# Seven products for every pair's second matrix, and the first MLP for all blocks ahead of the second

## The chip, the cores and the metric

The kernel runs on one core of a Trainium2 chip. The metric is device time in microseconds (us) from launch to end. The kernel before takes 1684.14 us, the median of three runs (1682.77, 1684.14, 1688.67).

## The reference

Attention over 8 batches, 8 heads, 576 tokens and head size 64, with a softmax of q over its features and a softmax of k over the sequence, is followed by two MLPs on 4608 tokens of width 512:

```python
x = attention(q, k, v)                       # 4608 x 512
x = relu(x @ w_in)**2 @ w_out                # w_in 512 x 2048, w_out 2048 x 512
x = (sigmoid(x @ w_gate) * (x @ w_val)) @ w_out2   # d_ff 1536
```

The weights arrive as float64. The result is float32.

## The kernel before, in words

**Arithmetic.** Each float32 operand is split into a rounded part and a rest (`hi_of` on ScalarE, L210, records of L211; `lo_of` on VectorE, L213, records of L214). `mm3` (L216) makes one product from three matmuls (L217 to L219). A seven-product form of Strassen's kind multiplies a 2x2 arrangement of blocks with seven products in place of eight: sums of operand blocks are made ahead (`plan_b` L673 and `b_comb` L669, records of L671, for activations; `plan_sums` L342 for weights), and each product's result is copied out of or added to an SBUF tile (`plan_seven` L762, records of L733, L211, L728). The order of the products is `PRODUCTS` (L137).

**Blocks and stages.** The tokens form nine blocks of 512. Blocks 0 to 2 go through the first MLP one at a time, beside the preparation of the first MLP's weights (until 366 us). The others go in pairs: `IN` is (3,4), (5,6), (7,8), called in0, in1, in2 here. `in_stage` (L1105) has two halves of the hidden width; in each, two units of seven products against w_in (`plan_in` L1036) are followed by the products against w_out. For these there are two forms. Eight products (L1158 to L1196, `o_mm` L854, `o_ev` L872): each of eight groups of the pair (4 `kk` in 2 halves) has four operand tiles split, and a weight tile that was fetched serves both blocks, 16 fetches of 0.5 MB a pair. Seven products (`out_seven` L1065, `p_o` L864): each group has seven tiles split and four sums made, each weight tile serves one product, 28 fetches, and the results of the second half are added to those of the first, loaded back (`o_ld7` L896). `OUT7` (L176) names the pairs that take seven. The first MLP's result goes to DRAM.

`GATE` is (0,1), (2,3), (4,5), (6,7), (8). `gate_stage` (L1200) loads a pair of blocks back and runs the second MLP on it, with seven products throughout.

**What sets the order.** Nothing is issued in the order of the loops. Every piece of work is put in a list with a key (a time in us by the plan's own clock), the engines that may do it and their costs, what it comes after, and which tiles it takes and gives back (`Plan.add` L44). `Plan.trace` (L55) runs through it as a list scheduler: an engine that is free takes the ready work with the lowest key for which tiles are there. The order that comes out is issued, and each engine's queue keeps it. A key is a priority, not an earliest time. Weight loads, weight fetches and the splits of a stage keep their own order by chains (L1309). `SIZES` (L177) gives the tiles: 11 of "W" for fetched and prepared weights and raw loads, 6 of "S" for split operands of the second matrices, 6 of "a" for attention's transposed q and for results on their way out, 5 of "w".

`STAGES` (L1275) is the order in which stages get their keys, one behind another from T1 = 358; a stage's length in keys is worked out from its matmuls. `BESIDE` (L1288) says beside which entry of `STAGES` the attention of which pair of blocks is planned (`plan_blocks` L1002; `plan_k` L601 and `plan_q` L622 give its steps). The nine matrices of the second MLP are prepared by `plan_w` (L390): each is four raw loads, a rounding of float64 to float32 words on ScalarE and VectorE (L250 to L284), four sums, seven splits and seven stores. Their keys are spread evenly from T4 = 299.6 to 40 past the start of the first gate stage (L1297).

Loads, fetches and stores are all issued by SyncE.

Of the kernel before, what the change touches and what calls it, by code (L numbers as in the profile page):

```python
# [29 lines left out]
class Plan:  # L30
# [13 lines left out]
    def add(self, key, engines, name, fn, *args, after=(), take=(), give=(), slack=0.0):  # L44
        n = len(self.ops)
        assert name not in self.names, name
        self.names[name] = n
        self.ops.append((key, n, engines, name, fn, args, tuple(after), tuple(take), tuple(give), slack))
# [94 lines left out]
def attention_mlp_mlp(  # L143
# [29 lines left out]
    F2 = w_out2.shape[0]  # L173
    wide = w_in.dtype == I64

    OUT7 = (2,)  # L176
    SIZES = {"X": 14, "W": 11, "S": 6, "f": 19, "x": 8, "q": 3, "a": 6, "w": 5, "k": 2, "v": 2, "km": 1, "kr": 2, "pa": 2, "qm": 4, "qr": 4}  # L177
    cst = ctx.enter_context(tc.tile_pool(name="cst", bufs=1))
    p4 = ctx.enter_context(tc.tile_pool(name="p4", bufs=1))
# [182 lines left out]
    def plan_first(kind, g, times, tag):  # L362

        ready, own = {}, {}
        for b in range(4) if kind == "in" else (0, 2, 1, 3):
# [5 lines left out]
            if kind == "in":  # L371
                add(t - 3.9, {DMA: 0.8}, ("w32", kind, g, b), w_store32, (kind, g, b), after=done)
                end.append(("w32", kind, g, b))
            if kind == "in" or not OUT7:
                add(t - 3, {FREE: 0.0}, ("wfre", kind, g, b), lambda: None, after=end, give=[tag])
# [297 lines left out]
    def plan_b(nm, ready, times, tag, n, gives):  # L673


        us = AS if n > 256 else 0.32
        ub = VEC if n > 256 else {DVE: 0.34}
        lo = lambda i: ("blo", nm, i)
        cb = lambda x: ("bcb", nm, x)

        def split(i, b, after, give=()):
            add(times[i], {ACT: us}, ("bhi", nm, i), b_hi, nm, i, b, tag, n, after=after, take=[tag])
            add(times[i] + 0.1, ub, lo(i), b_lo, nm, i, b, CHOSEN, after=[("bhi", nm, i)], give=give)

        def comb(x, i, o, a, b, after, give=()):
            add(times[i] - 1.5, ub, cb(x), b_comb, nm, o, a, b, CHOSEN, after=after, give=give)

        split(1, "11", ready["11"])
        comb("T1", 5, "11", "12", "11", [lo(1), *ready["12"]])
        split(5, "11", [cb("T1")])  # L690
        comb("T3", 7, "12", "22", "12", [cb("T1"), *ready["22"]])
        comb("T2", 6, "11", "22", "11", [lo(5), *ready["22"]])
        split(6, "11", [cb("T2")])
        split(2, "21", ready["21"])
        split(7, "12", [cb("T3")], gives.get("12", ()))
        split(3, "22", [*ready["22"], cb("T2"), cb("T3")], gives.get("22", ()))
        comb("T4", 4, "21", "21", "11", [lo(2), lo(6), cb("T2")], gives.get("11", ()))
        split(4, "21", [cb("T4")], gives.get("21", ()))
# [303 lines left out]
    def plan_blocks(js, t, per):  # L1002

        for j in js:
            new = [b for _, b in segs(j) if b not in done_b]
            done_b.update(new)
            for p in range(NP):
                for b in new:
                    plan_k(b, p, t, 1.0, x_before.get(j, []))
                plan_q(j, p, t + 2, 1.0)  # L1010
                t += per / NP
# [50 lines left out]
    IN = [tuple(range(j, j + 2)) for j in range(NONE, NB, 2)]  # L1062
    GATE = [(j, j + 1) for j in range(0, NB - 1, 2)] + [(NB - 1,)]
# [41 lines left out]
    def in_stage(n, t):  # L1105
# [5 lines left out]
        for h in range(2):  # L1111
# [15 lines left out]
            for kk in range(4):  # L1127
                nm = G + (kk,)
                if n not in OUT7:
                    continue  # L1130
# [9 lines left out]
                plan_b(nm, ready, times, "S", nt, {qn: ["f"] for qn in ready})  # L1140
            if n in OUT7:
                sorder.extend(("bhi", G + (kk,), i) for i in PRODUCTS for kk in range(4))
            for kk in range(4):
                if n in OUT7:
                    break
                for qn, (name, where) in gready[kk].items():
# [8 lines left out]
                    add(tk + 0.1, LOW, ("blo", nm, qn), b_lo, nm, qn, qn, CHOSEN, after=[("bhi", nm, qn)], give=["f"])  # L1155
            if n not in OUT7:
                sorder.extend([("bhi", G + (kk,), f"{r + 1}{tq + 1}") for tq in range(2) for kk in range(4) for r in range(2)])
            if n in OUT7:  # L1158
                t = out_seven(n, h, js, G, t)
# [112 lines left out]
        freed[prs[0]] = (t, fin)  # L1272
        return t

    STAGES = [(in_stage, 0), (in_stage, 1), (gate_stage, 0), (gate_stage, 1), (in_stage, 2), (gate_stage, 2), (gate_stage, 3), (gate_stage, 4)]  # L1275
    before = []
    for stage, n in STAGES:
        if stage is in_stage:
# [6 lines left out]
    plan_blocks([2], T2 + 6, TS1 * F1 - 30)  # L1285
    plan_blocks(IN[0], T3 + 5, (T1 - T3 - 40) / 2)

    BESIDE = {0: 1, 3: 2}  # L1288
    t = T1
    for i, (stage, n) in enumerate(STAGES):  # L1290
        if i in BESIDE:
            js = IN[BESIDE[i]]
            plan_blocks(js, t + 4, ((D1 if stage is in_stage else D2_) - 60) / len(js))
# [76 lines left out]
```

## Time and profile before

| | |
|---|---|
| median of three runs | 1684.14 us |
| the profiled execution's own time | 1689.22 us |
| its span, first to last instruction | 1687.4 us |
| mean granted TensorE clock | 0.992 |
| in0 (366.2 to 558.9 us), attention of blocks 5 and 6 beside it | 192.7 us |
| in1 (558.9 to 722.1 us) | 163.2 us |
| gate 0 (722.1 to 904.2 us) | 182.1 us |
| gate 1 (904.2 to 1096.8 us), attention of blocks 7 and 8 beside it | 192.6 us |
| in2 (1096.8 to 1248.3 us), seven products | 151.5 us |
| gate 2 (1248.3 to 1424.5 us) | 176.2 us |

Gates 3 and 4 follow until the end. The limits of the stages are the starts of their first matmuls; at some of them a few matmuls of two stages are interleaved. Busy time of an engine in a window is the union of its instructions' records. A window that shows an engine busy all the time does not say that it runs at its peak, since records of consecutive instructions overlap; the distance from start to start does.

### The profile page before, as it was taken

The page shows a single profiled execution, that of the slowest core. Times are in us where ns is not written, and L with a number is a line of the kernel's source. Part 1 is how long each engine was busy: PE and PEld are TensorE (multiplying, and loading weights), DVE is VectorE, ACT ScalarE, POOL GpSimd, SP SyncE. Part 2 cuts the span into 40 slices and gives each one's busy share as a digit, 9 for nine tenths or more (in the row PEclk, how much of TensorE's full clock was granted, in tenths as well). Part 3 has the DMA queues.
Part 4 walks back from the last instruction along what each step waited for, and adds up shares of the span by engine and source line. Part 5 has one row for each costly group of instructions (what it writes and reads, how often), then busy time and mean ns, then how long its engine had stood idle before and what let it go on. Part 6 is the DMA issues. An engine that isn't in the chain of part 4 may idle for free.

```text
span 1687.4 us, 24273 instructions
## 1 busy us (share of the span) xinstructions
PE 1651.6 (98%) x8740; PEld 1416.2 (84%) x8740; DVE 1158.9 (69%) x2178; ACT 927.6 (55%) x1632; POOL 1.9 (0%) x14
## 2 busy tenths in 40 slices
PE   6899999999999999999999999999999999999999
PEld 4677788878888888888898889988888899889998
DVE  8988846788889656865774758665954583448446
ACT  5876645567477657643454556464733453335344
POOL 0000000000000000000000000000000000000000
PEclk9998999999999999999999999999999999999999
DMA  7998899798897979899567555867786667555796
GB/s 287 343 359 327 305 360 334 278 342 343 298 347 256 369 256 351 303 335 355 188 191 243 191 186 164 274 201 250 243 291 195 191 210 240 191 196 185 246 377 253
DMA packets 153175, 457.90 MB, mean 271 GB/s; under 512 B 16096, under 2 KB 25312, under 8 KB 153056
## 3 DMA queue, kind: packets, MB, share of 16 engines
q1 hardware_dynamic: 153056, 456.36, 77.4%
q8 instruction: 69, 1.13, 0.3%
q14 instruction: 50, 0.41, 0.1%
HBM read 360.35 MB, written 95.94 MB: 270 GB/s over the span
## 4 chain that ended last, share of the span: by engine, by line
PE 90%; DVE 5%; DMA 2%; ACT 2%; issue 1%; SPq 0%; ACTq 0%; DVEq 0%
PE bank L217 29%; PE bank L219 28%; PE bank L218 28%; PE kps L467 2%; PE xps L577 2%; DMA ws<-w_in 1%; DVE bX L214 0%; DMA wraw<-in_moe_w_out_dram 0%; DVE whl L214 0%; DVE bS L214 0%; DMA kt<-in_k_dram 0%; DVE xf L671 0%; PE qsw L524 0%; DVE wf L277 0%; DVE s L671 0%
## 5 line engine op out<-in xcount | busy, mean ns | idle before, releaser
L217 PE MATMUL bank<-bX,ws 128*128 128x512 f32 (+1 forms) x1176 | 447.2, 380 | 3.2 <-DMA ws<-w_in 3.2
L218 PE MATMUL bank<-bX,ws 128*128 128x512 f32 (+1 forms) x1176 | 441.3, 375 | 0.0
L219 PE MATMUL bank<-bX,ws 128*128 128x512 f32 (+1 forms) x1176 | 441.2, 375 | 0.0
L733 DVE TENSOR_TENSOR s<-s,bank 128x512 f32<-128x512 f32 (+1 forms) x285 | 184.4, 652 | 206.6 <-PE bank L219 170.6
L211 ACT ACTIVATE s<-bank 128x512 f32<-128x512 f32 (+1 forms) x285 | 161.4, 570 | 225.9 <-PE bank L219 223.5
L217 PEld LDWEIGHTS bank<-bX,ws 128*128 128x128 f32 x1176 | 222.4, 189 | 42.3 <-ACT bS L211 3.5
L219 PEld LDWEIGHTS bank<-bX,ws 128*128 128x128 f32 x1176 | 222.1, 189 | 40.4
L218 PEld LDWEIGHTS bank<-bX,ws 128*128 128x128 f32 x1176 | 222.5, 189 | 37.9 <-issue 0.7
L211 ACT ACTIVATE bS<-s 128x512 fp32r<-128x512 f32 (+1 forms) x298 | 174.9, 598 | 124.4 <-PE bank L219 113.0
L214 DVE TENSOR_TENSOR bS<-s,bS 128x512 fp32r<-128x512 f32 (+1 forms) x298 | 191.6, 652 | 57.5 <-ACT bS L211 57.0
L217 PE MATMUL bank<-ws,bS 128*128 128x256 f32 x756 | 214.7, 284 | 0.0
L219 PE MATMUL bank<-ws,bS 128*128 128x256 f32 x756 | 214.1, 283 | 0.4 <-DVE bS L214 0.4
L218 PE MATMUL bank<-ws,bS 128*128 128x256 f32 x756 | 214.0, 283 | 0.0
L752 ACT ACTIVATE s<-s 128x512 f32<-128x512 f32 (+1 forms) x120 | 70.5, 589 | 140.2 <-DVE s L733 139.9
L217 PEld LDWEIGHTS bank<-ws,bS 128*128 128x128 f32 x756 | 145.0, 192 | 1.4 <-ACT s L211 0.3
L218 PEld LDWEIGHTS bank<-ws,bS 128*128 128x128 f32 x756 | 145.0, 192 | 1.0 <-issue 0.2
L219 PEld LDWEIGHTS bank<-ws,bS 128*128 128x128 f32 x756 | 145.0, 192 | 0.6 <-DVE bS L214 0.6
L217 PE MATMUL bank<-bS,ws 128*128 128x512 f32 x368 | 144.6, 393 | 0.2 <-issue 0.2
L218 PE MATMUL bank<-bS,ws 128*128 128x512 f32 x368 | 143.3, 389 | 0.0
L219 PE MATMUL bank<-bS,ws 128*128 128x512 f32 x368 | 143.3, 389 | 0.0
L211 ACT ACTIVATE whl<-wf 128x512 fp32r<-128x512 f32 x127 | 78.3, 626 | 50.1 <-DVE wf L284 27.8
L214 DVE TENSOR_TENSOR whl<-wf,whl 128x512 fp32r<-128x512 f32 x127 | 85.9, 689 | 10.1 <-ACT whl L211 9.9
(118 smaller groups left out, 2425.3 us busy)
## 6 DMA issues: line engine op xcount, KB each, us to landing
ws<-w_gv SPq DMA_DIRECT2D x210, 512.0 KB, 4.4
ws<-w_out SPq DMA_DIRECT2D x197, 512.0 KB, 4.3
ws<-w_in SPq DMA_DIRECT2D x116, 512.0 KB, 6.1
w_out<-whl SPq DMA_DIRECT2D x53, 512.0 KB, 4.7
w_gv<-whl SPq DMA_DIRECT2D x42, 512.0 KB, 6.2
w_in<-whl SPq DMA_DIRECT2D x32, 512.0 KB, 4.9
wraw<-in_moe_w_out_dram SPq DMA_DIRECT2D x28, 512.0 KB, 6.6
vt<-in_v_dram SPq DMA_DIRECT2D x32, 325.0 KB, 6.5
```

The costliest lines, as they stand in the source:

```text
L211: nc.scalar.activation(out=dst, in_=src, func=AF.Copy)
L214: by_name[engine].tensor_tensor(out=dst, in0=src, in1=hi.bitcast(F32), op=ALU.subtract)
L217: nc.tensor.matmul(ps, ah, bh, start=first, stop=False, skip_group_check=True)
L218: nc.tensor.matmul(ps, ah, bl, start=False, stop=False, skip_group_check=True)
L219: nc.tensor.matmul(ps, al, bh, start=False, stop=last, skip_group_check=True)
L467: nc.tensor.matmul(ps[:, 0:2 * D + 1], kt[:, r, :], vt[:, r, 0:2 * D + 1], start=(r == 0), stop=(r == RK - 1))
L577: nc.tensor.matmul(ps[:, e], kvf[b % 2][p], t[:, e], start=True, stop=True)
L733: nc.vector.tensor_tensor(out=t, in0=t, in1=banks[pr[b]][:, 0:n], op=ALU.add)
L752: nc.scalar.activation(out=t, in_=t, func=AF.Sigmoid)
```

## The change

`OUT7` names all three pairs, so in0 and in1 take seven products against w_out. `STAGES` puts the three in stages first and the five gate stages behind them. `BESIDE` plans the attention of blocks 7 and 8 beside in1 (entry 1) in place of gate 1 (entry 3). The keys of the nine matrices' preparation follow from the formula on L1297, which reads the start of the first gate stage.

```diff
-    OUT7 = (2,)
+    OUT7 = (0, 1, 2)
...
-    STAGES = [(in_stage, 0), (in_stage, 1), (gate_stage, 0), (gate_stage, 1), (in_stage, 2), (gate_stage, 2), (gate_stage, 3), (gate_stage, 4)]
+    STAGES = [(in_stage, n) for n in range(len(IN))] + [(gate_stage, n) for n in range(len(GATE))]
...
-    BESIDE = {0: 1, 3: 2}
+    BESIDE = {0: 1, 1: 2}
```

## Rows read from the trace of the kernel before

**Rows 1.** The page, part 1: busy time, share, instructions of each engine.
```profile
PE 1651.6 (98%) x8740; PEld 1416.2 (84%) x8740; DVE 1158.9 (69%) x2178; ACT 927.6 (55%) x1632; POOL 1.9 (0%) x14
```

**Rows 2.** The page, part 2: VectorE's busy tenths in 40 slices of 42.2 us.
```profile
DVE  8988846788889656865774758665954583448446
```

**Rows 3.** Waits of TensorE, 330 to 1690 us: total, times, longest.
```profile
PE bank L217 <- DMA ws<-w_in: 3.2, 1, 3.2
PE bank L217 <- DMA ws<-w_out: 1.2, 1, 1.2
```

**Rows 4.** Windows: length; busy PE, PEld, DVE, ACT, POOL; granted clock; DMA share, GB/s.
```profile
366.20:415.60 49.40, 46.25 (x208) 37.91 (x207) 36.52 (x74) 34.87 (x64) 0.00 (x0) 0.93 0.91 352
415.60:468.90 53.30, 53.30 (x264) 44.62 (x262) 46.85 (x105) 31.45 (x57) 0.00 (x0) 1.00 0.88 308
468.90:515.40 46.50, 46.50 (x231) 38.73 (x230) 38.16 (x83) 35.33 (x66) 0.00 (x0) 1.00 0.95 335
515.40:558.90 43.50, 43.50 (x194) 36.02 (x193) 36.77 (x64) 24.11 (x44) 0.00 (x0) 1.00 0.81 283
558.90:597.00 38.10, 38.10 (x170) 31.56 (x169) 23.50 (x38) 28.55 (x50) 0.00 (x0) 1.00 1.00 353
597.00:640.50 43.50, 43.50 (x194) 36.02 (x193) 26.07 (x45) 20.92 (x35) 0.00 (x0) 1.00 0.74 269
640.50:678.60 38.10, 38.10 (x170) 31.55 (x169) 26.47 (x45) 30.84 (x55) 0.00 (x0) 1.00 0.95 348
678.60:722.10 43.50, 43.50 (x194) 36.02 (x193) 35.12 (x61) 23.62 (x43) 0.00 (x0) 1.00 0.85 304
...
1096.80:1248.30 151.50, 151.26 (x668) 124.90 (x668) 100.73 (x161) 89.35 (x153) 0.00 (x0) 1.00 0.73 243
904.20:1096.80 192.60, 192.24 (x1114) 167.77 (x1113) 132.07 (x245) 104.53 (x164) 0.00 (x0) 1.00 0.63 208
1248.30:1424.50 176.20, 176.20 (x1016) 156.21 (x1015) 99.50 (x156) 75.49 (x125) 0.00 (x0) 1.00 0.66 212
722.10:904.20 182.10, 182.10 (x1045) 161.18 (x1043) 115.33 (x187) 85.86 (x143) 0.00 (x0) 1.00 0.75 264
```

**Rows 5.** Lines by form, VectorE: instructions that evict the first MLP's results.
```profile
L883 DVE TENSOR_TENSOR xp<-xp,bank 128x512 f32<-128x512 f32 x16 | 10.5, 692 | 6.2 <-DMA xp<-xp 4.8 <-PE bank L219 1.3
...
L733 DVE TENSOR_TENSOR xp<-xp,bank 128x512 f32<-128x512 f32 x14 | 9.0, 684 | 9.1 <-PE bank L219 9.1
...
L879 DVE COPY xo<-bank 128x512 f32<-128x512 f32 x6 | 4.1, 686 | 0.1
```

**Rows 6.** Timeline of VectorE in in0: start, length, operation, count.
```profile
528.38 1.90 DVE L214 TENSOR_TENSOR bX<-xf,bX 128x512 fp32r<-128x512 f32 x3
530.18 0.69 DVE L214 TENSOR_TENSOR whl<-wf,whl 128x512 fp32r<-128x512 f32 x1
530.78 0.43 DVE L264 TENSOR_SCALAR wf<-wf 128x512 f32<-128x512 f32 x1
531.12 0.70 DVE L671 TENSOR_TENSOR xf<-xf 128x512 f32<-128x512 f32 x1
```

**Rows 7.** Tile wraw on SyncE, raw loads: duration ns, first and last start.
```profile
L244 SPq DMA_DIRECT2D wraw<-in_moe_w_out_dram x28: 368/435/1072, 85.4 to 735.9; - x28
...
L244 SPq DMA_DIRECT2D wraw<-in_moe_w_gate_dram x12: 332/358/924, 318.7 to 575.8; - x12
```

**Rows 8.** Timeline of TensorE behind its longest wait in in0.
```profile
380.65 0.77 PE L217 MATMUL bank<-bX,ws 128*128 128x512 f32 x1 [3.15 <-DMA ws<-w_in]
...
385.91 0.62 PE L217 MATMUL bank<-bX,ws 128*128 128x512 f32 x1
386.33 0.43 PE L218 MATMUL bank<-bX,ws 128*128 128x512 f32 x1
386.60 0.40 PE L219 MATMUL bank<-bX,ws 128*128 128x512 f32 x1
386.83 0.39 PE L217 MATMUL bank<-bX,ws 128*128 128x512 f32 x1
```

## The prediction, made blind

> **What bounds the kernel now.** I first read the totals of the page: TensorE is busy 98% of the span, VectorE 69% [rows 1]. VectorE's forty slices say that 69% is a mean over unlike stages: it is at eight and nine tenths from the ninth slice to the thirteenth (337 to 548 us) and at four or five late in the run [rows 2]. TensorE's list of waits after 330 us has only two entries of 1 us or more, 4.4 us together, both for a fetched weight [rows 3]. So from there on the time is the number of matmuls times their spacing, as long as operands come in time. The table of windows then cuts the first two pairs of the first MLP (in0, in1) into their four phases each: seven products against w_in, eight products against w_out, and both again for the second half [rows 4]. In in1, 168 matmuls take 38.1 us and 192 take 43.5 us: 0.2266 us each with no idle time. In in0 the same phases are longer, since the attention of blocks 5 and 6 puts its own matmuls between. The last pair, in2, already takes seven products in both matrices; it runs at 151.5 us with TensorE busy 151.26, with VectorE at 100.7 us and neither attention nor weight preparation beside it [rows 4].
>
> **Matmuls.** Seven products instead of eight take 24 matmuls out of each half, 96 out of the two pairs: 96 x 0.2266 = 21.8 us, all on TensorE, which sets the end. An upper bound of the gain, because every other stage keeps its matmuls.
>
> **What VectorE gets for it.** Per pair, by the code: the eight-product form splits four tiles in each of eight groups (32 subtractions), the seven-product form seven (56): +24. Four sums per group: +32. Evictions: the eight-product form has 8 additions (16 in the two pairs) and 3 of its 8 copies on VectorE (6 of 16); the seven-product form has 6 additions in the first half, 14 in the second and about 2 copies: +11 [rows 5]. Together 67 instructions of 128x512 float32. Their price is the distance from start to start, not the recorded length: three in a row take 1.80 us from start to start, 0.60 each, and the next one again 0.60, though it is recorded as 0.69 [rows 6]. 67 x 0.60 = 40.2 us more VectorE work per pair, 20 us in each w_out phase, while that phase becomes 5.4 us shorter.
>
> The Trainium skill (VectorE: DVE Perf Modes, section "The DRAIN you can't avoid") says that the next operation does not start before the pipe of the one before is empty. By that rule the 67 would cost their recorded 0.69 us, 46.2 us a pair, and the forecast would be some 12 us higher; the trace here shows starts 0.60 us apart, and the measurement decides.
>
> **What is moved.** The preparation of the second MLP's weights is spread from a fixed point of the plan (T4 = 299.6) to 40 us past the plan's start of the first gate stage. That start moves from 704 to 843, since in2 now lies ahead of it and the other two are shorter (161.7 instead of 173.2 each). The nine matrices then come one per 64.8 us instead of 49.4. That such keys set the real pace shows in the loads: 36 of them between 318.7 and 735.9 us, 11.9 us apart where the plan asks 12.35, and not earlier although VectorE was idle for 52 us of in1 [rows 4, 7]. One matrix costs VectorE 4 blocks x (0.34 + 0.34 + 0.60 + 0.60) and 11 splits and sums x 0.60, 14 us (0.34 from start to start of the shorter kind [rows 6]). So each of in0 and in1 loses one matrix (3.5 to 2.5), 14 us, and in2 gains 35 us.
>
> The attention of blocks 7 and 8 moves from gate 1 to in1. Its price is the difference between two gate stages with and without it: TensorE 192.6 - 176.2 = 16.4 us, VectorE 132.07 - 99.50 = 32.6 us [rows 4]. On TensorE this is a move, net 0. On VectorE it leaves a stage at 0.69 load and enters one that has just been given 40 us.
>
> Its transposes also draw on the six tiles from which a seven-product half takes eight. No row shows the two together; the nearest is gate 1, where attention and eviction tiles share them and TensorE lost 0.36 us. Bounds: 0 to one product of 5.4 us in each of two w_out phases; I take 0 and keep the other end for the range.
>
> **ScalarE and SyncE.** 24 more splits per pair are 24 x 0.6 = 14 us for ScalarE; in1 has it busy 103.9 of 163.2 us [rows 4], so this is hidden. SyncE issues 12 more weight fetches of 0.5 MB per pair, +6.3 MB, and with one matrix less (4 loads, 7 stores) -5.8 MB. In0 moved 320 GB/s x 192.7 us = 61.7 MB and would move 62.2 MB in 181.8 us, 342 GB/s; in2 36.8 + 2.5 x 5.8 = 51.3 MB in 151.5 us, 339 GB/s. The first phase of in1 moved 353 GB/s without a wait, with the DMA share at 1.00 [rows 4]. I count 0, and a rival below. The second MLP's x2 loads and the fetch order of gates 2 to 4 are as before: 0. Gate 0 with 115.3 us of VectorE in 182.1 us has room: 0.
>
> **The balance.** In0: VectorE 158.3 + 40.2 - 14 = 184.5 us against 192.7 - 10.9 = 181.8 us of TensorE. In1: 111.2 + 40.2 - 14 + 32.6 = 170.0 against 163.2 - 10.9 + 16.4 = 168.7. In2: 100.7 + 35 = 136 against 151.5. So in0 and in1 ask for 354.5 us of VectorE in 350.5 us. If VectorE were never idle there, TensorE would still lose 4 us: the lower bound.
>
> The load is not even, though. By phases, with the preparation lighter by 3.5 us in each and the attention of in1 spread over the first three (11 us VectorE, 5.5 us TensorE each): in0 asks for 33, 63.4, 34.7 and 53.3 us in 49.4, 47.9, 46.5 and 38.1; in1 for 31, 53.6, 34 and 51.6 in 43.6, 43.6, 43.6 and 38.1. The w_out phases are over by 15.5, 15.2, 10 and 13.5, together 54 us; the w_in phases are under by 50. If nothing of the excess can use those gaps, TensorE loses 54 us: the upper bound. What can move is attention and preparation, up to what their buffers and keys allow; the splits cannot, since their inputs do not exist earlier and only six tiles hold them. The loads' even pace argues for little moving. I take the middle, 29 us, and one lost warm-up: after the one long wait of in0 (3.15 us) matmuls start 0.42 us apart instead of 0.23, and 13 of them take 5.7 us instead of 2.9 [rows 8]: the lower of the clock's two levels, 1.2 instead of 2.4 GHz, with the granted clock of that phase at 0.93 [rows 4]. That is 2.7 us. Sum: -21.8 + 29 + 2.7 = +10 us.
>
> The profiled execution took 1689.2 us, 5.1 above the median of the three runs, 1684.1. On it the sum gives 1699; on the median 1694, which I predict.
>
> **Rivals.** *Faster: the excess flows into the gaps.* Place: VectorE's queue in in0 and in1. If preparation and attention are ordered into the w_in phases, and the rest into in2 (15 us free) and gate 0, TensorE waits 4 to 10 us: 1684.1 - 21.8 + 8 = 1670. It decides once more than two thirds of the 54 us finds a gap: below a loss of 17 us the change is a gain beyond noise. For it: in0 before kept TensorE fed through a phase with VectorE at 46.85 of 53.3 us, and VectorE had stretches without a gap. Against: the even pace of the loads.
>
> *No change:* a loss of 17 to 27 us cancels the gain. 0.3% of the time, 5 us, is about what a measurement of this kernel can tell from none.
>
> *Slower still: DMA.* The prepared weights and the extra fetches leave 3 to 4% to the highest rate seen in a phase. The one long wait of in0 was for w_in [rows 3]; its price was 3.15 + 0.4 + 2.7, about 6 us. Two more of them on top of the forecast give 1694 + 12 = 1706.
>
> **Chances.** VectorE as forecast 0.42, DMA on top 0.14, so slower 0.56; no change 0.17; faster 0.27. The range reaches from 1668 (a loss of 6 us; some of the faster case lies below) to 1714 (a loss of 52 us, the upper bound).
>
> **What would show it.** Right: in0 and in1 take about as long as before or longer (in0 near 199, in1 near 181 us), TensorE's waits name VectorE's bS split inside their w_out phases, VectorE is above 0.95 there; in2 about 152 us; gate 1 shorter by 16 us. Wrong: in0 at 182 and in1 at 169 us with no TensorE waits (faster rival), or waits that name ws (DMA rival).

## The result, and the profile after

The changed kernel takes 1665.58 us (median of four runs, 1664.53 to 1672.16) against 1683.66 us before: 0.9891 of it, 95% interval 0.987 to 0.9912. It is faster by 18.1 us, where 10 us slower was forecast. A second series gave 1666.95 us and 0.9899 [0.9878, 0.992].

The profiled execution took 1665.63 us with a span of 1663.9. Its span is 23.5 us shorter than that of the profile before, more than the medians differ. In0 begins at 359.2 instead of 366.2 us, and that differs between runs of one kernel: from 150 to 200 us the granted clock was 0.86 in the profile before, 1.00 in this one and 0.90 in a second profile of the changed kernel. The stretch at the lower clock behind the one long wait of in0 [rows 8] is missing this time as well.

The page, part 1 and VectorE's forty slices:

```profile
PE 1625.4 (98%) x8644; PEld 1391.4 (84%) x8644; DVE 1224.7 (74%) x2307; ACT 939.1 (56%) x1672; POOL 2.0 (0%) x14
...
DVE  8999946779999999999797486347724683448446
```

TensorE has 96 matmuls fewer [rows 1], as counted. VectorE has 129 instructions more, and is at nine tenths in ten slices in a row, from the tenth (374 us) to the nineteenth, where it stood at five to nine before [rows 2].

TensorE's waits, 330 to 1690 us (total, times, longest):

```profile
PE bank L217 <- DMA ws<-w_in: 2.5, 2, 2.1
PE bank L218 <- DVE bS L214: 1.9, 4, 1.1
PE bank L217 <- DMA ws<-w_out: 1.1, 1, 1.1
PE bank L217 <- issue: 0.4, 1, 0.4
PE bank L217 <- ACT bS L211: 0.3, 1, 0.3
PE bank L217 <- ACT bX L211: 0.3, 1, 0.3
```

The wait that was forecast, on the split bS, is there, but it is 1.9 us long, not 29. All of them are 6.5 us.

Windows, with the columns of [rows 4]: first the phases of in0 (w_in; w_out; w_out mixed with the next w_in; the same for the second half), then in1's first w_in phase, then the stages from start to start, in0, in1, in2, gate 0 and gate 1. A stage starts with its first matmul, and that now lies up to 20 us before the last one of the stage ahead:

```profile
359.20:408.00 48.80, 46.53 (x219) 38.20 (x220) 35.70 (x77) 34.73 (x62) 0.00 (x0) 1.00 1.01 390
408.00:444.20 36.20, 36.20 (x178) 30.26 (x178) 35.70 (x75) 27.09 (x51) 0.00 (x0) 1.00 0.78 270
444.20:461.30 17.10, 17.10 (x84) 14.19 (x83) 16.73 (x35) 10.23 (x18) 0.00 (x0) 1.00 0.92 308
461.30:501.60 40.30, 40.30 (x204) 33.69 (x204) 38.57 (x85) 33.73 (x63) 0.00 (x0) 1.00 0.95 348
501.60:532.00 30.40, 30.07 (x132) 24.12 (x131) 30.25 (x52) 20.99 (x37) 0.00 (x0) 1.00 0.90 332
532.00:549.80 17.80, 17.80 (x80) 14.32 (x78) 17.80 (x32) 10.56 (x19) 0.00 (x0) 1.00 0.96 345
549.80:585.30 35.50, 35.50 (x174) 29.29 (x173) 34.93 (x76) 28.41 (x53) 0.00 (x0) 1.00 0.97 343
...
359.20:531.90 172.70, 170.10 (x810) 140.40 (x811) 156.86 (x320) 126.66 (x227) 0.00 (x0) 1.00 0.92 337
531.90:702.90 171.00, 169.80 (x776) 137.84 (x775) 167.39 (x327) 123.65 (x222) 0.00 (x0) 1.00 0.88 309
702.90:858.20 155.30, 153.67 (x673) 125.77 (x672) 137.10 (x232) 110.71 (x195) 0.00 (x0) 1.00 0.94 346
858.20:1032.30 174.10, 174.10 (x961) 152.54 (x961) 122.66 (x199) 82.21 (x138) 0.00 (x0) 1.00 0.77 263
1032.30:1207.20 174.90, 174.90 (x1011) 155.11 (x1010) 99.42 (x156) 73.79 (x123) 0.00 (x0) 1.00 0.67 214
```

VectorE (the third busy column) is full in the w_out phases, as forecast: 35.70 of 36.20 and 30.25 of 30.40 us. TensorE is full all the same, and the w_in phases have VectorE at 0.96 and 0.98 where it had 0.82 and 0.62 [rows 4] (the second of them now has attention beside it). The third and the sixth row have no like in in0 and in1 before, where the next w_in matmuls start behind the last w_out one: here TensorE takes w_out and w_in matmuls by turns. The timeline shows one such turn:

```profile
531.71 0.39 PE L219 MATMUL bank<-bS,ws 128*128 128x512 f32 x1
531.94 0.39 PE L217 MATMUL bank<-bX,ws 128*128 128x512 f32 x1
...
533.07 0.39 PE L219 MATMUL bank<-bX,ws 128*128 128x512 f32 x1
533.30 0.39 PE L217 MATMUL bank<-bS,ws 128*128 128x512 f32 x1
...
534.43 0.39 PE L219 MATMUL bank<-bS,ws 128*128 128x512 f32 x1
534.66 0.39 PE L217 MATMUL bank<-bX,ws 128*128 128x512 f32 x1
```

Six matmuls of the next pair's first products (bX), six of this pair's last (bS), and again, without a gap. Such a turn needs a new split tile bS every 2.7 us instead of every 1.36. Between 531.9 and 549.8 us it happens six times, and at the end of every other w_out phase alike.

The raw loads answer [rows 7]:

```profile
L244 SPq DMA_DIRECT2D wraw<-in_moe_w_out_dram x28: 383/449/1187, 87.4 to 864.1; - x28
...
L244 SPq DMA_DIRECT2D wraw<-in_moe_w_gate_dram x12: 327/337/592, 314.0 to 655.3; - x12
```

### The profile page after: what moved, and what is told of

It reads as the page before. It is cut to its first block, busy times and chain, and to the rows that moved or that the text cites. A ratio compares the mean times of both kernels' runs of the same rounds, so it can differ in the third digit from the quotient of the medians.

```text
span 1663.9 us, 24397 instructions
## 1 busy us (share of the span) xinstructions
PE 1625.4 (98%) x8644; PEld 1391.4 (84%) x8644; DVE 1224.7 (74%) x2307; ACT 939.1 (56%) x1672; POOL 2.0 (0%) x14
## 4 chain that ended last, share of the span: by engine, by line
PE 88%; DVE 6%; ACT 3%; DMA 2%; issue 1%; SPq 0%; DVEq 0%; ACTq 0%
PE bank L217 28%; PE bank L219 28%; PE bank L218 28%; PE kps L467 2%; PE xps L577 2%; DVE bS L214 1%; DMA ws<-w_in 1%; DMA qt<-in_q_dram 1%; DVE bX L214 1%; DVE whl L214 0%; DVE xp L733 0%; PE qsw L524 0%; DVE s L671 0%; DVE wf L284 0%; DMA w_gv<-whl 0%
## 5 line engine op out<-in xcount | busy, mean ns | idle before, releaser
L219 PE MATMUL bank<-bX,ws 128*128 128x512 f32 (+1 forms) x1176 | 440.1, 374 | 0.0
L733 DVE TENSOR_TENSOR s<-s,bank 128x512 f32<-128x512 f32 (+1 forms) x297 | 191.4, 654 | 216.2 <-PE bank L219 177.6
L211 ACT ACTIVATE s<-bank 128x512 f32<-128x512 f32 (+1 forms) x297 | 168.4, 572 | 213.5 <-PE bank L219 210.3
L211 ACT ACTIVATE bS<-s 128x512 fp32r<-128x512 f32 (+1 forms) x330 | 194.8, 601 | 132.0 <-PE bank L219 112.5
L214 DVE TENSOR_TENSOR bS<-s,bS 128x512 fp32r<-128x512 f32 (+1 forms) x330 | 214.5, 656 | 62.6 <-ACT bS L211 62.1
L219 PEld LDWEIGHTS bank<-bX,ws 128*128 128x128 f32 x1176 | 221.4, 188 | 40.0
L219 PE MATMUL bank<-ws,bS 128*128 128x256 f32 x756 | 213.9, 283 | 0.0
L219 PEld LDWEIGHTS bank<-ws,bS 128*128 128x128 f32 x756 | 145.1, 192 | 0.0
L217 PE MATMUL bank<-bS,ws 128*128 128x512 f32 x336 | 134.2, 400 | 1.3 <-issue 0.4
L218 PE MATMUL bank<-bS,ws 128*128 128x512 f32 x336 | 131.4, 391 | 1.9 <-DVE bS L214 1.9
L219 PE MATMUL bank<-bS,ws 128*128 128x512 f32 x336 | 131.1, 390 | 0.0
L671 DVE TENSOR_TENSOR s<-s,s 128x512 f32<-128x512 f32 (+1 forms) x192 | 122.2, 655 | 1.7 <-ACT s L739 0.2
```

The lines of the kernel that those rows point to most:

```text
L211: nc.scalar.activation(out=dst, in_=src, func=AF.Copy)
L214: by_name[engine].tensor_tensor(out=dst, in0=src, in1=hi.bitcast(F32), op=ALU.subtract)
L217: nc.tensor.matmul(ps, ah, bh, start=first, stop=False, skip_group_check=True)
L218: nc.tensor.matmul(ps, ah, bl, start=False, stop=False, skip_group_check=True)
L219: nc.tensor.matmul(ps, al, bh, start=False, stop=last, skip_group_check=True)
L671: by_name[engine].tensor_tensor(out=t[o], in0=t[a], in1=t[b], op=ALU.subtract)
```

## The experiments

All changes are to the changed kernel unless it says otherwise. "Theory" and "rival" were written ahead of each run. The ratio and the interval are to the kernel before, measured beside each run. What a run costs or gains against the changed kernel is taken from the changed kernel's 1665.58 or 1666.95 us; a difference under some 4 us cannot be told from none.

**1. The two halves of the change, each alone.** First the order of stages with eight products kept:

```diff
-    OUT7 = (0, 1, 2)
+    OUT7 = (2,)
```

> The new order of stages, with the eight-product form kept in in0 and in1 (OUT7 = (2,)). Theory (TensorE's matmuls set the time, and the order only makes room for VectorE): the matmuls are those of the kernel before, VectorE asks for 158 - 14 = 144 us in in0's 193 us and 111 - 14 + 33 = 130 us in in1's 180 us, so nothing is short and nothing is won: 1684 us, within 5 us of the kernel before. Rival (the order saves by itself, through fewer changes between stages): 1678 us or less, and then the seven products gave less than their 21.8 us.

Measured: 1681.94 us, 0.9992 [0.9979, 1.0005]. The order alone brings nothing. Then seven products in the old order, a change to the kernel before:

```diff
-    OUT7 = (2,)
+    OUT7 = (0, 1, 2)
```

> Seven products for all three pairs, in the order of stages of the kernel before, attention of blocks 7 and 8 beside gate 1. Theory (VectorE's balance matters, the new order buys the room): the preparation keeps its old pace, so in0 asks VectorE for 158 + 40 = 198 us in 182 us of TensorE and in1 for 111 + 40 = 151 us in 152; the 16 us of excess have no free stage beside them and show as waits of TensorE on split operands: 1672 to 1682 us, 7 to 16 us above the changed kernel. Rival (VectorE's queue gives way at no cost, the order is idle): 1663 to 1669 us, as the changed kernel.

Measured: 1710.75 us, 1.0154 [1.0132, 1.0177]: 27 us slower than before, 45 slower than with both. So neither half gains, and the seven products need the order. The loss was larger than either expectation. The window of its in0:

```profile
363.40:571.30 207.90, 184.00 (x836) 149.69 (x836) 192.05 (x381) 138.72 (x250) 0.00 (x0) 0.94 0.84 313
```

The timeline of TensorE at its longest wait, and that of SyncE ahead of it:

```profile
538.67 0.39 PE L219 MATMUL bank<-bS,ws 128*128 128x512 f32 x1
548.72 0.77 PE L217 MATMUL bank<-bS,ws 128*128 128x512 f32 x1 [9.66 <-ACT wraw L260]
549.28 0.63 PE L218 MATMUL bank<-bS,ws 128*128 128x512 f32 x1
549.71 0.63 PE L219 MATMUL bank<-bS,ws 128*128 128x512 f32 x1
```

```profile
522.93 1.37 SPq L307 DMA_DIRECT2D ws<-w_out  x3
533.68 8.74 SPq L302 DMA_DIRECT2D w_gv<-whl  x2
542.52 0.38 SPq L244 DMA_DIRECT2D wraw<-in_moe_w_gate_dram  x1
542.95 2.32 SPq L307 DMA_DIRECT2D ws<-w_out  x4
```

In0 takes 207.9 us with VectorE busy 192. The wait is put down to a ScalarE copy of raw weights (L260), but the matmul does not read what that copy writes. By the order of the splits its own tile was ready at 539.63 us; the fetched weight that it also waited for landed at 548.59, 0.13 us before it started. SyncE issued that fetch at 542.95, since it had stood from 524.4 to 542.1 us at two stores of prepared weights that VectorE had still to split (the splits end at 533.62 and 542.04). From 520 to 575 us such stores held it longest (total, times, longest):

```profile
SPq L302 <- DVE whl L214: 24.5, 5, 9.3
```

So VectorE's lateness reaches TensorE through SyncE's queue here. Of TensorE's 36.8 us of waits behind 355 us, 33 end within 0.2 us of the landing of a fetched weight, though the DMA share in in0 is only 0.84. Nor does the order give TensorE work of the next pair to turn to: that pair's x is split from 536 to 565 us, against 520 to 548 in the changed kernel, and in0 ends with one turn of the two kinds of matmuls instead of six. Behind the 9.66 us matmuls start 0.43 us apart, at the lower clock; the granted clock of the stage is 0.94.

**2. The phases kept apart.** The w_in products of a unit, and the first of gate 0, wait for the last w_out matmul before them:

```diff
+        barrier = list(last_out)
+        last_out.clear()
...
-                    after=[("wf", use), ("blo", xn + (0,), i), ("blo", xn + (1,), i)] + (wait[m:m + 1] if i not in OPENS else wait),
+                    after=[("wf", use), ("blo", xn + (0,), i), ("blo", xn + (1,), i)] + barrier + (wait[m:m + 1] if i not in OPENS else wait),
...
+            last_out[:] = [nm]
```

> The changed kernel with one dependency more: the w_in products of the unit behind a w_out phase wait for that phase's last matmul, so the two no longer mix on TensorE. Same instructions. Theory (the excess of the w_out phases was absorbed because the plan mixes the next unit's w_in products into their last quarter, which halves the rate at which split operands are needed): TensorE waits on VectorE's bS in the w_out phases, 10 to 50 us in all, 1676 to 1715 us, likeliest 1688. Rival (attention and preparation gave way inside VectorE's queue, the mixing is a by-product): 1664 to 1670 us.

Measured: 1682.50 us, 0.999 [0.9976, 1.0005]: 17 us of the 18 are gone. Its TensorE waits, 355 to 900 us:

```profile
PE bank L218 <- DVE bS L214: 8.3, 10, 1.8
PE bank L217 <- ACT bS L211: 3.9, 2, 2.1
PE bank L217 <- DMA ws<-w_in: 2.0, 1, 2.0
```

They name the split, at ten places and two. The w_out phase at the end of in0 has VectorE full and is 5.6 us longer than the 38.1 us that its 168 matmuls take:

```profile
505.80:549.50 43.70, 39.84 (x169) 31.03 (x168) 43.17 (x74) 28.88 (x51) 0.00 (x0) 1.00 0.91 325
```

As a control the same dependency went into the kernel of the order alone, where in0 and in1 have eight products:

```diff
                     freed[pr] = (t - 3 + 3 * oh, ends)
+                    last_out[:] = [("o", n, h, tq, oh, 3)]
```

> The kernel of the order alone (eight products in in0 and in1) with the phases kept apart, as in the run that did so with seven. Theory (keeping the phases apart costs only where a w_out phase asks VectorE for more than it has; with eight products none of in0 and in1 does): 1680 to 1686 us, within 4 us of the order alone. Rival (mixing helps any kernel here, for another reason such as weight fetches): 1690 to 1700 us, as much as the 17 us that it cost with seven products.

Measured: 1686.09 us, 1.0014 [0.9998, 1.003], 4 us above the order alone, with intervals that overlap; in2 has seven products there too and loses its mixing. So mixing is worth much only where a w_out phase asks VectorE for more than it has.

**3. Dose and response: the pace of the preparation.** The spread of the nine matrices, by the plan's keys:

```diff
-                plan_w(kind, g, T4 + (t + 40 - T4) / len(preps) * m, 10.0, "w")
+                plan_w(kind, g, T4 + (T1 + 2 * D1 + 40 - T4) / len(preps) * m, 10.0, "w")
```

> The changed kernel with the nine matrices prepared at the old pace (one per 49.4 us by the plan's keys instead of 64.8), all else as changed. Theory (in0 and in1 have VectorE full, so work added there lengthens them): 14 us more of VectorE work in each, 28 us in all, less what slips behind: 1675 to 1693 us, TensorE waiting on bS or bX. Rival (VectorE still has room, its high load is work pulled forward): 1663 to 1669 us.

Measured: 1698.07 us, 1.009 [1.0073, 1.0106], 32 us for one matrix more (14 us of VectorE) in each of in0 and in1. Its trace has 26.5 us of TensorE waits behind 355 us against 6.5, and behind the longer ones 41 matmuls of 512 columns take 0.39 to 0.47 us from start to start instead of 0.23, against 5, some 7 us more: together 27 of the 32. Of the waits 6.9 us name the split bS, and 13 end with a fetched weight that has just landed; SyncE's stores of prepared weights wait 82 us for VectorE there (355 to 900 us) and 46 in the changed kernel. With `t - 30` in place of `t + 40`:

> The changed kernel with one matrix per 57.1 us of the plan's keys, between the changed kernel's 64.8 (1666 us) and the 49.4 that gave 1698 us. Theory (in0 and in1 are full, every us of VectorE work added there lengthens them by as much or more): half of the way, 1678 to 1686 us. Rival (a knee: there is room up to a point, and late operands of the next pair then cost all at once): 1666 to 1672 us.

Measured: 1676.58 us, 0.9969 [0.9953, 0.9986], between the two expectations. With `t + 90`:

> The changed kernel with the preparation spread 50 us further (one matrix per 70.4 us of the plan's keys instead of 64.8). Theory (what the changed kernel still loses, some 4 us, is VectorE's excess in in0 and in1): 3 us less of VectorE work in each, 1661 to 1665 us, faster than the changed kernel by 1 to 4 us. Rival 1 (nothing is left to win, the last matrices become late for gate 0): 1666 us or more, with TensorE waiting in gate 0. Rival 2: no difference, within 1 us.

Measured: 1663.40 us, 0.9886 [0.9871, 0.99]. The four paces, 49.4, 57.1, 64.8 and 70.4 us per matrix, give 1698, 1677, 1666 and 1663 us: the curve is steep where the stages are overfull and flat where they fit. Each pace also gives an order of its own, and what that alone does was not tested here. The changed kernel and the later pace were run again side by side:

> The changed kernel again, beside the later pace on one chip, to settle what the later pace is worth: 1664 to 1667 us.

> The later pace (one matrix per 70.4 us) again. Theory (a few us of VectorE's excess are left in the changed kernel): 1 to 4 us below the changed kernel beside it. Rival: within 1 us of it.

Measured: 1666.95 (0.9899 [0.9878, 0.992]) and 1662.75 us (0.9875 [0.9855, 0.9896]). The later pace was ahead by 2 and by 4 us, with intervals that overlap: the fastest kernel here, its lead over the changed one not settled.

**4. Is it additive?** Seven products in in1 and in2 alone:

```diff
-    OUT7 = (0, 1, 2)
+    OUT7 = (1, 2)
```

> The new order with seven products in in1 and in2 only (OUT7 = (1, 2)), eight in in0. Theory (each pair's seven products are worth 48 matmuls x 0.2266 = 10.9 us as long as VectorE keeps up): halfway, 1671 to 1675 us. Rival (in0, with the larger attention beside it, is where the gain is lost, in1 gives its full share): 1666 to 1669 us, so that in0's seven products bring next to nothing.

Measured: 1672.05 us, 0.9936 [0.9915, 0.9956]. From eight products through one pair to two it goes 1681.9, 1672.0, 1665.6: 9.9 us from in1 and 6.4 from in0, of 10.9 each.

**5. Which engine?** At the old pace, one VectorE operation was left out, the one that sets the weights' sign (so the second MLP's weights come out positive):

```diff
-            add(t + 0.3, {DVE: TT}, ("wg",) + key, w_sign, key, after=[("wb",) + key])
+            last = "wb"
+            if kind not in ("gv", "out2"):
+                last = "wg"
+                add(t + 0.3, {DVE: TT}, ("wg",) + key, w_sign, key, after=[("wb",) + key])
```

> The kernel with the old pace of preparation (1698 us), without the VectorE operation that sets the sign of the nine matrices of the second MLP (their weights come out positive): 36 operations of 0.60 us, about 17 us of VectorE work less in in0 and in1, with every load, store, fetch and ScalarE operation as before. Theory (VectorE's work binds at the old pace): most of the loss goes, 1674 to 1684 us. Rival (the raw loads, the tiles that they hold or ScalarE bind): 1692 us or more.

Measured: 1687.14 us, 1.0022 [1.0012, 1.0032]. Between the two: 11 of the 32 us came back for some 17 us of VectorE work. Then work was added to the changed kernel without a change of its order, on ScalarE:

```diff
         nc.scalar.activation(out=low, in_=low.bitcast(U32), func=AF.Copy, scale=2.0**-29)
+        for _ in range(2 if key[0] in ("gv", "out2") else 0):
+            nc.scalar.activation(out=low, in_=low.bitcast(U32), func=AF.Copy, scale=1.0)
```

> The changed kernel with two idle copies more on ScalarE for each raw block of the nine matrices (72 operations of 0.55 us, some 11 us in each of in0, in1 and in2, more than the 8 us of ScalarE work that the old pace added to in0 and to in1), in the same order. Theory (VectorE binds, ScalarE has room): 1664 to 1670 us. Rival (ScalarE's queue, which holds the first half of every split, binds): 1675 us or more.

Measured: 1676.84 us, 0.9954 [0.9939, 0.9969]. The rival's number: it cost 10 us, though ScalarE is at 0.73 in in0. The work was more than expected: each copy works on what the one before it wrote, and from start to start the two add 1.41 us to a raw block, 51 us in all. So VectorE alone could not be the whole answer, and the same was done on VectorE:

```diff
-        nc.vector.tensor_scalar(out=t, in0=t, scalar1=E_MIN, scalar2=E_MAX, op0=ALU.max, op1=ALU.min)
+        for _ in range(4 if key[0] in ("gv", "out2") else 1):
+            nc.vector.tensor_scalar(out=t, in0=t, scalar1=E_MIN, scalar2=E_MAX, op0=ALU.max, op1=ALU.min)
```

> The changed kernel with three idle repeats of VectorE's clip for each raw block of the nine matrices (108 operations of 0.34 us, some 10 us in each of in0, in1 and in2, as much as the idle copies on ScalarE were), in the same order. Theory (VectorE is full in in0 and in1, so its work there lengthens the span one for one): 1682 to 1692 us, 17 to 25 us over the changed kernel. Rival (any work put into the preparation's chain delays what is queued behind it, whichever engine does it): about 10 us over it, 1673 to 1680 us, as the copies on ScalarE cost.

Measured: 1704.94 us, 1.0113 [1.0091, 1.0134], 38 us over the changed kernel and more than either expectation. The work was more than expected here as well. The timeline of VectorE shows four clips of one block and what follows them:

```profile
405.20 1.79 DVE L265 TENSOR_SCALAR wf<-wf 128x512 f32<-128x512 f32 x4
406.91 0.68 DVE L734 TENSOR_TENSOR s<-s,bank 128x512 f32<-128x512 f32 x1
```

The clips, each on the tile that the one before it wrote, start 0.46 us apart, not 0.34. Four take 1.72 us to the next instruction's start where one takes 0.34, so 36 blocks got 50 us of VectorE work in place of 37, and 50 us cost 38. In2, where the forecast saw room, became 6.5 us longer too; there VectorE is at 137.10 of 155.30 us in the changed kernel. The window over the three stages of this kernel:

```profile
360.00:880.00 520.00, 493.69 (x2215) 396.71 (x2216) 489.11 (x952) 351.60 (x630) 0.00 (x0) 0.99 0.87 315
```

Some 50 us of work in the preparation of the same blocks cost 38 us on VectorE and 10 on ScalarE: four times as much. VectorE binds; the preparation's chain, which passes through ScalarE too, may add to it. At the old pace without the sign the trace still shows 19.8 us of waits and 40 such slow matmuls; which part of them is VectorE's stays open.

**6. Where is VectorE's work free?** Two controls in gate 1, with the order unchanged. First 35 subtractions done twice:

```diff
-        lo_of(hl[:, 1], bq[nm][b], hl[:, 0], engine)
+        for _ in range(2 if nm[0] == "X2" and nm[1] == 2 or nm[0] == "Y" and nm[1] == 1 and nm[2] % 2 else 1):
+            lo_of(hl[:, 1], bq[nm][b], hl[:, 0], engine)
```

> The changed kernel with 35 of the subtractions of gate 1 (14 of the next pair's x, 21 of y) done twice, 21 us of VectorE work more in a stage that lasts 175 us and has VectorE at 0.57. Theory (VectorE's work costs only where it is full): within 3 us of the changed kernel, 1663 to 1670 us. Rival (work in a queue whose order was planned without it delays TensorE anywhere): 1673 us or more.

Measured: 1682.93 us, 0.9992 [0.9979, 1.0005]: 16 us for 25 us of work (a subtraction done twice takes 1.33 us from start to start, done once 0.60). The stage's mean had misled: the split of y comes in a burst. The window of the changed kernel there:

```profile
1158.00:1175.00 17.00, 17.00 (x142) 16.96 (x141) 17.00 (x29) 9.69 (x17) 0.00 (x0) 1.00 0.64 205
```

TensorE's longest waits in the control (total, times, longest):

```profile
PE bank L219 <- DVE bS L214: 7.5, 2, 4.0
```

Then 72 idle clips in the first part of the stage, where VectorE is at 0.48:

```diff
+    def idle(uid, t):
+        for _ in range(3 if uid[:2] == ("u2", 1) else 0):
+            nc.vector.tensor_scalar(out=t, in0=t, scalar1=-1e30, scalar2=1e30, op0=ALU.max, op1=ALU.min)
```

> The changed kernel with three idle clips behind each of gate 1's 24 products of sigmoid and value, 72 operations of 0.34 us, 24 us of VectorE work in the 125 us of its first part, where VectorE is at 0.48, in the same order. The run before this one put 21 us into the same stage but into its second part, where VectorE is at 1.00 for 17 us, and cost 16 us. Theory (what counts is whether VectorE is full in the stretch): within 3 us of the changed kernel, 1663 to 1670 us. Rival (the fixed order makes any added work cost): 1675 us or more.

Measured: 1675.45 us, 0.9947 [0.993, 0.9964]: 9 us, and neither expectation holds. These clips too start 0.46 us apart; with the wait for the product ahead of them they add 1.38 us each time, 33 us in all. Windows of this kernel, of the first part and of the start of the second:

```profile
1045.00:1150.00 105.00, 105.00 (x477) 87.37 (x475) 72.40 (x134) 38.24 (x64) 0.00 (x0) 1.00 0.64 201
1150.00:1175.00 25.00, 18.96 (x109) 17.59 (x108) 23.79 (x43) 9.89 (x19) 0.00 (x0) 0.80 0.45 151
```

Its timeline there, with the one long wait that the changed kernel does not have (L219 needs the split that VectorE makes):

```profile
1167.54 0.58 PE L219 MATMUL bank<-ws,bS 128*128 128x256 f32 x1 [6.04 <-DVE bS L214]
1167.92 0.41 PE L217 MATMUL bank<-ws,bS 128*128 128x256 f32 x1
1168.13 0.41 PE L218 MATMUL bank<-ws,bS 128*128 128x256 f32 x1
```

For 105 us the added work is free: VectorE is at 0.69 and TensorE never waits. The last unit's clips, ahead of the burst of splits, are what costs: 6.04 us of waiting and then matmuls of 256 columns 0.21 us apart instead of 0.12, at the lower clock (0.80 over the window).

## Why the prediction was wrong, point by point

- **Matmuls**: right. 96 fewer; 21.8 us is the upper bound, and 18.1 of it came.
- **VectorE's 67 instructions a pair**: right within a few. The split subtractions rose by 48 and the sums by 64 over two pairs, in all 129 instead of 134. The price of 0.60 us, and not the recorded 0.69, holds where neighbours work on different tiles: the splits of the changed kernel from 1158 to 1175 us start 0.60 us apart. It does not hold for the added clips, 0.46 us apart in place of 0.34 with records of 0.43. The Trainium skill (VectorE: DVE Perf Modes, section "The DRAIN you can't avoid") lets an operation start only when the pipe of the one before is empty, and adds that one that is not held starts earlier. The 0.60 us with records of 0.69 do not agree with the first half alone; the clips do.
- **The moves**: right. The 36 raw loads run from 314.0 to 864.1 us, 15.7 us apart (16.2 by the plan's keys). Gate 1 became 17.7 us shorter (16.4 forecast).
- **DMA**: right at 0 for this kernel. TensorE's waits on ws are 3.6 us in all (4.4 before), with the DMA share at 0.88 to 0.94 in the three stages. With seven products alone, fetched weights did hold TensorE for 33 us, by the order of SyncE's queue and not by the rate, which is where the forecast looked.
- **The balance**: right in kind, not in size. It asked for 354.5 us of VectorE in in0 and in1 against 350.5 of TensorE. From in0's first matmul to in2's the two took 343.7 us, with VectorE busy 324.3 (0.94), 30 us less than asked for. Some of the rest falls behind in2's first matmul, which lies 19 us before in1's last, and gate 0 has 7 us more than before. And the sum added work at prices from start to start to busy times by records, in which an instruction that stands alone counts 0.69: the page's total rose by 65.8 us, not 80.4.
- **The step that failed**: "the splits cannot, since their inputs do not exist earlier and only six tiles hold them. The loads' even pace argues for little moving. I take the middle, 29 us". The loss was 21.8 - 18.1 = 3.7 us (0 to 7 by the interval). That it meets the lower bound of 4 us is luck, since the balance behind that bound asked for up to 30 us too much. I had cut TensorE's work into phases that follow each other, and held each against VectorE's work of the same phase. The plan is not bound to them: at the end of each w_out phase TensorE takes w_out and next w_in products by turns. That halves the w_out phase's demand in its last quarter and hands VectorE's excess to the w_in phase behind it, where VectorE stood at 0.96 and 0.98; the forecast had 34.7 of 46.5 us there and 31 of 43.6. Keeping the phases apart cost 17 us.
- **The rest of the 54 us**: with the phases kept apart the loss is 20.6 us (1682.5 against 1683.7 - 21.8), not 54, and the w_out phase at the end of in0 is over by 5.6 us, not by 15.2. So some 33 us never showed, even without any mixing. Some of such work moved inside VectorE's queue, which the step had called unlikely: in that kernel VectorE is busy 44.14 of 45.00 us in in1's first w_in phase (549.5 to 594.5 us). Some, by the balance, was not there. How the 33 us divide stays open. The pace of the raw loads, which I took as evidence, tells how far ahead preparation runs, not what TensorE does meanwhile.
- **Why the plan mixes**: not because splits are late. The trace before shows the same turns in in2, from 1160.7 to 1171.6 us, with VectorE idle:

```profile
1160.70 0.39 PE L217 MATMUL bank<-bX,ws 128*128 128x512 f32 x1
...
1162.06 0.39 PE L217 MATMUL bank<-bS,ws 128*128 128x512 f32 x1
...
1163.42 0.39 PE L217 MATMUL bank<-bX,ws 128*128 128x512 f32 x1
```

```profile
1160.70:1171.60 10.90, 10.90 (x50) 9.03 (x49) 1.23 (x3) 2.90 (x5) 0.00 (x0) 1.00 0.84 291
```

The turns come with the seven-product form; eight products have none in in0 and in1. By the code, each product of `out_seven` comes after the one before it, which the plan counts as done 0.2 us late (`LATENCY`, L35), and a next w_in product that is ready goes in between. This is read from the code and was not tested. That the turns fall where VectorE is short was this change's luck, and the forecast could have read them in in2.

- **The warm-up of 2.7 us**: did not occur; the granted clock was 1.00 in every phase.
- **The rivals**: the faster one came, near its 1670 us. Its mechanism, work that moves inside VectorE's queue, can account for up to 33 of the 54 us; alone that would have left the 20.6 us of the rival "no change". The 17 us that made it a gain came from TensorE's order, which no rival named. That DMA would bind fell in this kernel.
- What the forecast saw rightly, that VectorE is at its limit, shows only where the room is taken away: 50 us of work added to it cost 38, and seven products without the new order are 27 us slower than before.

## What to carry to other kernels

Where a scheduler orders the work, hold two engines' sums against each other over the whole stretch in which their work can be reordered, not phase by phase, and look in the trace for work of the next phase that already mixes in. An engine at 0.95 can cost next to nothing as long as its results come in time, and work added to it then cost three quarters of its length here: so measure the slope, not the load. Price added work from its own trace: an instruction on the tile that the one before it wrote takes longer from start to start than one beside it. And before a wait is put down to the engine that it names, look when everything that it waits for was ready. A mean over a stage says nothing of room: where a burst stands at 1.00, added work costs at once.

## What the runs showed of the hardware

VectorE ran at 1.00 for 17.8 us and at 0.99 or more for 48 us on end (501.6 to 549.8) while TensorE waited 0.33 us. Clips of 128x512 on the tile that the clip before wrote start 0.46 us apart on VectorE, where a clip followed by other work takes 0.34. Waits of 9.66 us (matmuls 0.43 us apart behind it instead of 0.23) and 6.04 us (0.21 instead of 0.12) were followed by matmuls at the lower clock; those of the changed kernel behind 359 us, 2.1 us and less, were not: its granted clock is 1.00 in every stage. The length of the wait alone does not decide it: behind 2.01 us in the kernel with the copies on ScalarE matmuls soon started 0.43 us apart, and behind 2.41 us at the old pace 0.23. The engine that a wait names can be another than the one that is late: the 9.66 us are put down to a ScalarE copy that ended at 548.60 us, and a fetched weight had landed at 548.59, 5.6 us after its issue.
